# Two token tiles loaded by halves, one behind a weight tile, and work moved within and off VectorE's queue, in an attention and feed-forward kernel

## The chip, the cores and the metric

The kernel runs on one core of a Trainium2 chip. Its engines each have a queue of their own: TensorE (PE) multiplies and transposes, VectorE (DVE), ScalarE (ACT) and GpSimd (POOL) do elementwise work, and SyncE (SP) issues most of the transfers; ACT and POOL can issue transfers too. The metric is the device time of one execution in microseconds (us). A profiled execution also has a span, from its first instruction to its last.

## The reference, cut to what matters

```python
xn = layernorm(x)                                   # x: 1 x 2048 x 448
qkv = xn @ wqkv                                     # 448 x 1344; 16 heads of 28
# attention over 8 keys, 2 positions apart: idx = pos - (0, 2, ..., 14), masked where idx < 0
attn = softmax(where(mask, einsum("bhsd,bhswd->bhsw", q, kg) * 28 ** -0.5, -1e9))
s = einsum("bhsw,bhswd->bhsd", attn, vg).reshape(1, 2048, 448) @ wo
g = silu(gelu(xn @ w1 + b1) @ w2 + b2)              # 448 x 1792 and 1792 x 448
out = x + s * g
```

The kernel computes all of it in bfloat16 with float32 sums.

## The kernel before, in words

**Tiling.** The 2048 tokens, even positions first and odd ones behind, are 16 token tiles of 128 rows (in SBUF: `x_sb`). The 448 columns of the model are contracted in row tiles (`kt`) of 128, the last of 64. So `wqkv` comes in row tiles 0, 1 and 2 (`w_in[:, kt]`) and a last one of 64 rows (`w_in3`). The load of row tile 2 stands ahead of that of row tile 1.

**Stages.** For each token tile VectorE takes the statistics (`stats`: BN_STATS L354, BN_AGGR L358), gets the reciprocal deviation with ACT or POOL (`rstds`), and writes the normalized tile `xn` (L422) with a copy of its last 64 columns behind it (L427). It is turned into `xnT`: for tiles 0 to 3 by PE (L404, L437) with a copy out of PSUM by DVE or ACT (`copy`, L250 and L252), for the others by a transposing transfer that SP issues (`dma_T`, L301). From `xnT` PE makes rows of q and k (L513) and v (L536). They are cast out of PSUM by ACT (L250) or DVE (L252) into `qk_tok` or `qk_pair` and `v_tok`; the first two are turned into `qkT` by transfers, v is written to DRAM and read back as windows. The first products, for tiles 0 and 1, are ordered by row tile of the weights: 0, 2, 1, and the last (`first_batch`). The feed-forward is L589 (`ff1`) with a GELU on ACT (L593) and L615 or L641 (`ff2`), to which DVE adds the second bias (`y`, L657).

Attention works on blocks of queries. `keys` makes `kb`, the keys of a block masked by plane (L700 on DVE, L698 on ACT, two instructions each); `scores` multiplies them (L715), ACT takes the exp (`E`, L721), and DVE or POOL multiplies by the mask (L731); `values_sum` multiplies E with v (L746), and DVE divides (`rd` L757, `a` L762). `a` goes through DRAM into `oT`. `store` multiplies the output product (L780, L795) by the gate (`sg`, L803 or L805), adds x (`o`, L811) and sends it out (L815).

**What sets the order.** Every step is a task added to a plan with the engines it may run on. `ORDER` is the program: a list of task numbers, each with the letter of the engine that it goes to (P, V, A, G, S for PE, DVE, ACT, POOL, SP; D marks where a transfer may count as landed). `emit` writes the instructions in that order, so on each engine they run in it, one behind the other. Buffers (8 PSUM banks, 4 `xn`, 2 `y`, 2 `kb`, 2 `sg`, 3 `o`) are taken and given back at the places in the list. Products by pairs of 64 rows (`pair`) have a small signal between their halves, issued by POOL, SP or ACT.

At the start the list has eleven matmuls on constants (L265, ten of 512 columns and one of 128), which depend on no load. A transfer from SP or ACT uses one of eight semaphores in turn; the ninth waits until the first has landed.

Of the kernel before, what the change touches and what calls it, by code (L numbers as in the profile page):

```python
# [11 lines left out]
ACT = mybir.ActivationFunctionType  # L12
# [10 lines left out]
G140 D141 V152 P301 V153 G297 V91 S154 D155 P163 G302 V89 P298 V90 G164 V92 V87 G94 G264 G265 D266 P303 A300 V143 P165
V79 A305 S144 D145 P316 V194 A166 V198 A299 V195 G167 D168 P311 V199 S196 D197 V80 V88 V169 G317 G93 A304 P318 S200
D201 P306 A319 G312 V186 G170 D171 V187 V190 A320 G172 D173 P313 V191 S188 D189 G307 G174 D175 P156 V653 A314 G176
D177 V654 P308 A315 S192 D193 G157 G178 D179 P158 A310 P291 V159 A160 S256 D257 S258 D259 A309 P321 G292 S262 D263
G180 D181 S260 D261 P293 G322 G182 D183 P225 A294 P323 A295 G226 P227 A325 P267 P485 V229 A324 V273 S161 D162 P505
A228 G486 V275 V277 V279 P487 G506 V274 P495 A488 V276 V268 A489 P507 G496 V278 V280 P497 V282 A509 P475 V284 V286
A508 V283 V285 A498 P209 V288 G476 G210 V287 G281 A499 P477 V289 P216 V334 G217 G290 A478 V335 V338 S336 D337 P211
A479 V339 V330 P480 V213 S340 D341 V212 P218 V326 G481 P490 A219 V327 V331 S214 D215 A222 G220 D221 P482 G491 G223  # L30
D224 V683 P492 A484 S332 D333 V684 P500 A493 V412 A483 P202 V413 S328 D329 G501 A494 V400 P502 G203 V401 S402 D403
P204 A504 P655 V205 P580 A503 V206 S207 D208 S414 D415 A50 G248 D249 V408 G250 D251 V409 A656 V404 P239 A658 A581 V405
V657 V659 S410 D411 P582 G240 S230 D231 S406 D407 P660 V586 P685 A661 P241 V583 A663 P232 V245 V662 A686 P365 V713
V664 A688 G233 V714 A587 P234 A366 V687 V689 A242 P690 G923 V236 P367 A235 V588 P589 A691 S237 D238 G243 D244 A693
V692 V694 G246 D247 A584 S924 D925 A369 V585 S926 D927 A368 P715 S370 D371 G590 P695 P665 V696 A716 P591 V666 V697
A718 V667 V698 V668 V699 V669 G700 D701 P349 V592 G670 D671 S672 D673 P720 V595 A593 G350 P674 G702 D703 P351 V675
A721 G252 D253 V676 P416 A352 G254 D255 V353 A723 P342 G417 V677 S354 D355 V678 A596 P418 G343 V743 G679 D680 P704
V717 A420 P344 G681 D682 V705 A419 V706 P598 A346 S421 D422 V719 V707 A345 V708 V744 G709 D710 S347 D348 V597 G711
D712 P725 V722 G599 P745 V726 P750 V727 A746 P600 S928 D929 A748 V728 V729 A751 V724 G730 D731 S732 D733 A753 V594
V747 V749 P734 V604 P379 V735 A605 V736 P372 G380 V737 P381 V738 G373 P356 V601 G741 S739 D740 D742 A385 S930 D931  # L40
V773 A602 P755 G386 D387 P374 V756 G357 V382 P358 A375 V757 G383 D384 P430 A359 V774 A362 P446 G360 D361 V758 V759
G363 D364 P775 V376 S447 S760 D761 P448 G431 G762 D763 G388 D389 G392 D393 A776 V752 S377 D378 P780 A778 V449 P432
A781 V754 P423 S424 V803 A783 P764 V777 A450 P425 V765 A433 V766 P453 G390 D391 A436 V767 V768 P607 A427 V426 A454
S769 D770 G394 D395 V779 G396 D397 V804 G398 D399 V606 G434 D435 V603 G437 D438 P455 V782 G608 P439 V784 G771 D772
G271 D272 G269 D270 A459 V456 P805 G460 D461 V833 A440 P441 A806 G457 D458 V834 P785 A808 P609 V786 A443 V787 V788
V789 G463 D464 G465 D466 V442 S792 S428 D429 G790 D791 D793 V807 V809 S444 D445 G462 P810 V613 P540 A811 V610 A813
A541 P794 P815 V812 A51 G467 D468 P515 V795 V796 G469 D470 P542 V797 A516 V798 A611 P517 V816 G801 S799 D800 D802 V817
A544 P530 V818 A543 V819 P535 V814 A518 A531 G820 D821 V612 G822 D823 P824 A614 P532 A536 G471 D472 A519 V825 P537
V826 G473 D474 A534 P510 V827 V828 A539 V615 V863 P525 G829 D830 S831 D832 A533 A511 A538 P512 S526 A864 P520 P955
S521 S451 D452 A514 P527 G956 A513 P957 A528 P522 V958 V959 A529 P944 V962 A524 V963 P835 P840 A523 G945 S960 D961  # L50
P946 S964 D965 A52 P616 V947 V951 V952 A841 S953 D954 A843 V842 V948 A836 P865 V844 S949 D950 S934 D935 S932 D933 S936
D937 G617 P870 A838 V837 P618 A871 V839 A873 G872 A866 A868 V867 G874 A893 P845 V622 P625 G869 V846 V847 A623 V848
A894 V849 V619 G850 D851 V624 P854 G852 D853 A620 S626 P895 P627 V855 A896 V856 A898 V857 V858 V621 G859 D860 V897
G861 D862 V899 P550 V631 V628 P966 A632 G551 A629 V633 P900 G967 P977 A901 V630 A903 P968 V902 G978 A53 V904 P545 S938
D939 V973 P979 V974 G546 V969 S975 D976 P552 V980 G970 P905 A554 P547 V906 V907 S971 D972 A553 P555 V908 V981 A549
V909 S982 D983 P875 G556 P557 A548 V984 S910 D911 P884 S912 D913 V876 A559 P575 V877 A558 V885 P570 V886 S576 V887
V888 P577 S571 V878 G889 D890 P572 V879 A578 G891 D892 V985 P999 A579 G880 D881 S986 D987 P560 A574 G1000 G882 D883
# [66 lines left out]
def kernel(  # L124
# [13 lines left out]
    P = 128  # L138
# [17 lines left out]
    for v in range(9):  # L156
        n = NW - 1 if v == 4 else NW
# [23 lines left out]
    x_sb = sb("x_sb", [P, NT, D])  # L181
# [38 lines left out]
    p_st = ring("st", 4, [P, 6], F32)  # L220
# [38 lines left out]

    t_on = plan.add("DMA", lambda _: None, ())  # L260
    t_warm = t_on
    for n in (512,) * 10 + (P,):
        def idle(k, n=n):
            one = nc.const_aps
            nc.tensor.matmul(buf(p_b, k)[:, :n], one.tensor(1.0, [P, P], BF16), one.tensor(1.0, [P, n], BF16), start=True, stop=True)  # L265
        t_warm = plan.add("PE", idle, [t_warm], take=(p_b,))
        t_warm.give = ((p_b, t_warm, 0),)
# [18 lines left out]
    def dma(eng, dst, src, deps=()):  # L286
        def fn(_):
            {"SP": nc.sync, "ACT": nc.scalar, "POOL": nc.gpsimd}[eng].dma_start(dst, src)
        a = plan.add(eng, fn, [t_on] + list(deps))
        return plan.add("DMA", lambda _: None, [a])  # L290
# [61 lines left out]
    def stats(t):  # L352
        def f1(k):
            nc.vector.bn_stats(out=buf(p_st, k)[:], in_=x_sb[:, t, :])  # L354
# [578 lines left out]
    t = plan.add("POOL", None, [seen[b, 1][0] for b in range(2)])  # L933
# [43 lines left out]
```

## Time and profile before

| | |
|---|---|
| median of 3 runs | 149.83 us (149.45 to 150.26) |
| the profiled execution | 149.96 us |
| its span | 148.2 us |
| granted TensorE clock | 0.997 |
| instructions | 4658 |

A profile's row has the start in us, the length in us (merged rows: from the first start to the last end), engine and line, operation, output and inputs with their sizes, and the count; in brackets the idle time of the engine just before it and what ended it. A group's row has after the bar the busy us, the mean ns of one, and behind the second bar the idle time before them. A window's row has, for each engine, its busy us in that stretch, then PE's clock, the share of the DMA engines and GB/s. SPq is SP's queue: its transfers are listed by when they are issued and how long the issue takes. L12 is line 12 of the kernel.

### The profile page before, as it was taken

Reading aid. Unit: us, or ns where it says so; the run is one execution under the profiler, and the core shown is the slowest. Engines: PE = TensorE matmul, PEld = TensorE weight load, DVE = VectorE, ACT = ScalarE, POOL = GpSimd, SP = SyncE. Lnnn points to the kernel's source line nnn. Section 1 sums busy time; section 2 is a strip of 40 time slices with the busy share of each in tenths; the row PEclk is TensorE's granted clock in tenths of the full one; section 3 lists DMA queues with packets and bytes.
Section 4 is the critical chain, followed back from the end, with each engine's and each line's share of the span. In section 5 each row is a group of like instructions: output and inputs, shape, how many; then the busy total and the mean of one; then the engine's idle time right before and its main releaser. Section 6 shows DMA issues by size and latency. Waiting matters only on the chain.

```text
span 148.2 us, 4658 instructions
## 1 busy us (share of the span) xinstructions
PE 142.9 (96%) x1827; PEld 78.7 (53%) x1827; DVE 108.2 (73%) x302; ACT 89.2 (60%) x164; POOL 56.0 (38%) x112
## 2 busy tenths in 40 slices
PE   7899999999999899999999999999999999999991
PEld 2444555444455566666665554545665564545570
DVE  3789934198941997999999999627589997671642
ACT  4336676675782682645574539989874876571120
POOL 6753694007330021651389675600463024110200
PEclk9999999999999999999999999999999999999998
DMA  4999999999599899697489989952682332264112
GB/s 145 320 282 323 189 205 193 255 367 206 143 154 130 179 132 192 133 198 181 117 227 136 215 203 122 300 113 64 102 176 78 71 98 63 78 166 127 43 31 62
DMA packets 43966, 24.17 MB, mean 163 GB/s; under 512 B 33822, under 2 KB 42022, under 8 KB 43944
## 3 DMA queue, kind: packets, MB, share of 16 engines
q1 hardware_dynamic: 41080, 17.25, 59.4%
q0 software_dynamic: 2720, 6.51, 17.9%
q8 instruction: 14, 0.23, 0.7%
q10 hardware_dynamic: 144, 0.11, 0.2%
q14 instruction: 8, 0.07, 0.1%
HBM read 9.70 MB, written 6.29 MB: 108 GB/s over the span
## 4 chain that ended last, share of the span: by engine, by line
PE 64%; DMA 17%; DVE 12%; SPq 2%; issue 2%; POOL 1%; DVEq 0%
PE bank L615 18%; PE bank L589 14%; PE bank L513 10%; PE bank L641 7%; DMA xnT<-xn 6%; PE bank L780 5%; DMA w_in<-in_A_wqkv_dram 4%; DMA qkT<-qk_tok 4%; PE bank L536 4%; DVE st L354 3%; DMA x_sb<-in_A_x_dram 3%; PE bank L746 3%; PE bank L715 2%; DVE qk_tok L252 2%; PE bank L795 1%
## 5 line engine op out<-in xcount | busy, mean ns | idle before, releaser
L589 PE MATMUL bank<-xnT,w 64*128 64x512 bf16 x392 | 46.6, 376 | 0.0
L593 ACT ACTIVATE h<-bank,b 128x512 bf16<-128x512 f32 x56 | 35.2, 686 | 13.6 <-PE bank L589 13.2
L615 PE MATMUL bank<-w,h 64*128 64x448 bf16 x336 | 33.8, 349 | 0.0
L589 PEld LDWEIGHTS <-w 64*128 64x128 bf16 x392 | 19.7, 94 | 19.5 <-issue 0.6
L513 PE MATMUL bank<-w_in,xnT 64*128 64x448 bf16 (+1 forms) x212 | 26.3, 350 | 0.6 <-DVE y L657 0.4
L615 PEld LDWEIGHTS <-h 64*128 64x128 bf16 x336 | 17.1, 94 | 12.9
L721 ACT ACTIVATE E<-bank 128x456 bf16<-128x456 f32 (+1 forms) x36 | 17.4, 550 | 10.6 <-PE bank L715 9.5
L769 POOL DMA_DIRECT2D o_rows<-a x25 | 13.4, 538 | 26.4 <-DVE a L762 10.2
L762 DVE TENSOR_TENSOR a<-bank,rd 114x448 bf16<-114x448 f32 (+1 forms) x36 | 22.2, 622 | 1.1
L295 POOL DMA_DIRECT2D v<-v_rows x22 | 13.9, 637 | 7.0 <-PE bank L589 6.5
L513 PEld LDWEIGHTS <-xnT 64*128 64x128 bf16 (+1 forms) x212 | 10.9, 94 | 9.1 <-issue 1.2
L295 POOL DMA_DIRECT2D v_rows<-v_tok x16 | 9.1, 572 | 14.5 <-PE bank L715 9.4
L536 PE MATMUL bank<-w_in,xnT 64*128 64x448 bf16 (+1 forms) x106 | 13.8, 349 | 0.0
L657 DVE TENSOR_TENSOR y<-bank,b 128x448 f32<-128x448 f32 x15 | 9.0, 620 | 5.7 <-PE bank L641 4.8
L354 DVE BATCH_NORM_STATS2 st<-x_sb 128x6 f32<-128x448 bf16 x16 | 9.2, 610 | 3.9 <-DMA x_sb<-in_A_x_dram 3.9
L731 DVE TENSOR_TENSOR E<-E,m_gen 128x456 bf16<-128x456 bf16 (+1 forms) x29 | 10.8, 393 | 1.4 <-ACT E L721 1.4
L641 PE MATMUL bank<-w,h 128*128 128x448 bf16 (+2 forms) x70 | 11.4, 315 | 0.0
L669 ACT ACTIVATE t<-y 128x448 f32<-128x448 f32 x12 | 6.9, 579 | 7.3 <-DVE y L657 7.3
L700 DVE TENSOR_SCALAR kb<-qkT,plane 128x512 bf16<-128x512 bf16 x30 | 9.1, 352 | 2.8 <-DMA qkT<-qk_tok 1.9
L422 DVE TENSOR_SCALAR xn<-x_sb,mv,rstd 128x448 bf16<-128x448 bf16 x15 | 5.8, 393 | 6.2 <-DMA xnT<-xn 4.2
L250 ACT CAST v_tok<-bank 128x448 bf16<-128x448 f32 x12 | 6.2, 540 | 6.6 <-PE bank L536 4.2
L252 DVE CAST qk_tok<-bank 128x448 bf16<-128x448 f32 x11 | 6.5, 617 | 2.9 <-PE bank L513 2.9
(86 smaller groups left out, 170.7 us busy)
## 6 DMA issues: line engine op xcount, KB each, us to landing
v_rows<-v_tok POOLq DMA_DIRECT2D x16, 128.0 KB, 3.2
v<-v_rows POOLq DMA_DIRECT2D x14, 128.0 KB, 5.0
out_dram<-o SPq DMA_DIRECT2D x15, 112.0 KB, 1.7
w<-in_B_w_dram SPq DMA_DIRECT2D x2, 784.0 KB
o_rows<-a POOLq DMA_DIRECT2D x23, 64.1 KB, 3.2
w<-in_B_w_dram SPq DMA_DIRECT2D x2, 672.0 KB
x_sb<-in_A_x_dram SPq DMA_DIRECT2D x3, 448.0 KB, 7.2
w_in<-in_A_wqkv_dram SPq DMA_DIRECT2D x3, 336.0 KB, 4.9
```

The source lines that it names most:

```text
L295: nc.gpsimd.dma_start(dst(k), src())
L354: nc.vector.bn_stats(out=buf(p_st, k)[:], in_=x_sb[:, t, :])
L513: return nc.tensor.matmul(ps[:, :D], xnT[r, kt, cs], w, start=start, stop=stop)
L536: return nc.tensor.matmul(ps[:, :D], xnT[r, kt, k0:k0 + P], w, start=start, stop=stop)
L589: return nc.tensor.matmul(ps[:], w1[r, kt, ms], xnT[r, kt, cs], start=start, stop=stop)
L593: nc.scalar.activation(buf(p_h, own, i)[:], buf(p_b, own, i)[:], ACT.Gelu_apprx_tanh, bias=b1[:, mt:mt + 1])
L615: return nc.tensor.matmul(ps[:, :D], buf(*h_at[(c, mt)])[r, j * P:(j + 1) * P], w2[r, mt, :], start=start, stop=stop)
L641: nc.tensor.matmul(ps[:, :n], buf(*h_at[(c, mt)])[:, j * P:(j + 1) * P], w2[:, mt, cs], start=(mt == 0 and not biased), stop=(mt == NMT - 1))
L721: nc.scalar.activation(buf(p_E, k)[:, :n], buf(p_b, a, r)[:, :n], ACT.Exp, scale=SCALE)
L731: (nc.gpsimd if k.on == "POOL" else nc.vector).tensor_tensor(out=E, in0=E, in1=m, op=ALU.mult)
L762: nc.vector.tensor_tensor(out=o, in0=sums(k, e)[:, :, :, :DH], in1=buf(p_rd, rd)[rows].unsqueeze(2).unsqueeze(3).to_broadcast((2 * nq, 8, ...
L769: (nc.gpsimd if k.on == "POOL" else nc.sync).dma_start(o_rows[n + i * nq:n + i * nq + nq, :], buf(p_a, own)[i * nq:i * nq + nq, i, :])
```

## The change

It has two parts, in the loads at the start and in the list of tasks.

**Loads.** Token tiles 0 and 1 are each loaded by two transfers of 64 rows, the first half on SP and the second on ACT (before: tile 0 whole on SP, tile 1 whole on ACT). Tiles 2 and 3, one transfer before, are two, and that of tile 3 stands behind row tile 1 of the weights. The statistics of a tile wait for both of its halves. The matmuls on constants are ten instead of eleven.

SP's queue from the program's start, before the change (`w_in` 128x1344 is a row tile of `wqkv`, row tile 0 and then 2 in the second row and row tile 1 in the fourth; `w_in_65` the last row tile; `w_66` is `w1`):

```order
L288 DMA x_sb<-in_A_x_dram 128x448
L288 DMA w_in<-in_A_wqkv_dram 128x1344 x2
L288 DMA x_sb<-in_A_x_dram 128x2x448
L288 DMA w_in<-in_A_wqkv_dram 128x1344
L288 DMA w_in_65<-in_A_wqkv_dram 64x2x448
L288 DMA w_in_65<-in_A_wqkv_dram 64x896
L288 DMA w_66<-in_B_w_dram 128x3x896
```

And after it:

```order
L288 DMA x_sb<-in_A_x_dram 64x448 x2
L288 DMA w_in<-in_A_wqkv_dram 128x1344 x2
L288 DMA x_sb<-in_A_x_dram 128x448
L288 DMA w_in<-in_A_wqkv_dram 128x1344
L288 DMA x_sb<-in_A_x_dram 128x448
L288 DMA w_in_65<-in_A_wqkv_dram 64x2x448
L288 DMA w_in_65<-in_A_wqkv_dram 64x896
L288 DMA w_66<-in_B_w_dram 128x3x896
```

The load of two tiles has become one load before and one behind row tile 1, and two halves stand where one tile stood. ACT's queue begins with two halves instead of one tile.

**The list.** Two xn with their copies (V408 V409 and V404 V405 before) go behind the masks of the first exps, and the second of them behind the two y. Five casts (before V353, V382, V376, V426, V442) and three pairs of kb (V744, V804, V834) go from DVE to ACT, and one sum o (V959) from DVE to POOL. Since five more load tasks are made and one matmul task fewer, a task's number from the weights' later loads on is greater by 5.

DVE's queue at 45 to 51 us of the profile, before (`y_104` is the y that frees the bank of the next q product; `E<-E,m_first` are the first masks):

```order
L252 CAST qk_pair<-bank_159 128x16x28
L252 CAST qk_pair<-bank_161 128x16x28
L422 TENSOR_SCALAR xn<-x_sb,mv,rstd 128x448
L427 COPY xn<-xn 128x64
L422 TENSOR_SCALAR xn<-x_sb,mv,rstd 128x448
L427 COPY xn<-xn 128x64
L731 TENSOR_TENSOR E<-E,m_first 128x456 x2
L657 TENSOR_TENSOR y_104<-bank_156,b_72 128x448
L657 TENSOR_TENSOR y_105<-bank_155,b_72 128x448
L252 CAST v_tok_78<-bank_159 128x16x28
```

And after:

```order
L252 CAST qk_pair<-bank_158 128x16x28
L252 CAST qk_pair<-bank_160 128x16x28
L735 TENSOR_TENSOR E<-E,m_first 128x456 x2
L426 TENSOR_SCALAR xn<-x_sb,mv,rstd 128x448
L431 COPY xn<-xn 128x64
L661 TENSOR_TENSOR y_104<-bank_155,b_72 128x448
L661 TENSOR_TENSOR y_105<-bank_154,b_72 128x448
L426 TENSOR_SCALAR xn<-x_sb,mv,rstd 128x448
L431 COPY xn<-xn 128x64
L252 CAST v_tok_78<-bank_158 128x16x28
```

The masks stand first, and the y ahead of the second xn. The lines after the load helper are 4 greater; the bank numbers are shifted by one all through, since one matmul fewer takes a bank at the start.

ACT's queue at 61 to 69 us, before:

```order
L250 CAST qk_pair_150<-bank3_157 128x16x28
L721 ACTIVATE E_98<-bank7_161 128x456
L669 ACTIVATE t1_107<-y1_105 128x448
L250 CAST qk_tok1_152<-bank0_154 128x16x28
L250 CAST qk_tok1_152<-bank6_160 128x16x28
L250 CAST qk_pair_150<-bank4_158 128x16x28
L250 CAST qk_pair_150<-bank2_156 128x16x28
L721 ACTIVATE E_98<-bank3_157 128x456
```

And after:

```order
L250 CAST qk_pair_150<-bank2_156 128x16x28
L250 CAST qk_pair_150<-bank4_158 128x16x28
L725 ACTIVATE E_98<-bank6_160 128x456
L673 ACTIVATE t1_107<-y1_105 128x448
L250 CAST qk_tok1_152<-bank7_161 128x16x28
L250 CAST qk_tok1_152<-bank5_159 128x16x28
L250 CAST qk_pair_150<-bank3_157 128x16x28
L250 CAST qk_pair_150<-bank1_155 128x16x28
L702 ACTIVATE kb1_149<-qkT_74,plane_82 128x2x4x64 x2
L725 ACTIVATE E_98<-bank2_156 128x456
```

A second cast of `qk_pair` stands ahead of the first exp and a pair of kb ahead of the next four.

The diff, with a line of the list for the start:

```diff
 ORDER = """
-D0 A31 D32 G14 S29 D30 V12 P1 V13 V15 V19 V20 A48 V21 S33 D34 V22 V16 G45 V17 V18 P2 V23 G46 D47 S39 D40 P3 S35 D36
+D0 A30 D31 G13 S28 D29 S32 D33 A34 D35 V11 P1 V12 V14 V18 V19 A53 V20 S36 D37 V21 V15 G50 V16 V17 P2 V22 G51 D52 S44
...
     t_warm = t_on
-    for n in (512,) * 10 + (P,):
+    for n in (512,) * 9 + (P,):
...
+    def load_x_halves(t):
+        t_x[t] = [dma(eng, x_sb[r:r + 64, t, :], rows(x_half, t * P + r, 64), ()) for eng, r in (("SP", 0), ("ACT", 64))]
+
     def load_x(t0, n, eng="SP", deps=()):
         d = dma(eng, x_sb[:, t0:t0 + n, :], rows(x_half, t0 * P, n * P).rearrange("(t p) d -> p t d", p=P), deps)
         for t in range(t0, t0 + n):
-            t_x[t] = d
+            t_x[t] = [d]
...
-    load_x(0, 1, "SP")
-    load_x(1, 1, "ACT")
+    load_x_halves(0)
+    load_x_halves(1)
...
     load_w(0)
-    load_x(2, 2, "SP")
+    load_x(2, 1, "SP")
+    load_x(3, 1, "SP")
     load_w(1)
...
-        k = plan.add("DVE", f1, [t_x[t]], take=(p_st,))
+        k = plan.add("DVE", f1, t_x[t], take=(p_st,))
```

More of the change, by code (lines that the diff above doesn't have):

```diff
@@ L23 @@
[L23 to L57, printed above, removed]
@@ new lines @@
+V287 A514 P480 V289 V291 A513 V288 V290 A503 P214 V293 G481 G215 V292 G286 A504 P482 V294 P221 V339 G222 G295 A483
+V340 V343 S341 D342 P216 A484 V344 V335 P485 V218 S345 D346 V217 P223 V331 G486 P495 A224 V332 V336 S219 D220 A227
+G225 D226 P487 G496 G228 D229 V688 P497 A489 S337 D338 V689 P505 A498 V417 A488 P207 V418 S333 D334 G506 A499 V405
+P507 G208 V406 S407 D408 P209 A509 P660 V210 P585 A508 V211 S212 D213 S419 D420 A55 G253 D254 G255 D256 A661 P244 A663
+A586 V662 V664 V413 V414 S415 D416 P587 G245 S235 D236 P665 V591 P690 A666 P246 V588 V409 V410 S411 D412 A668 P237
@@ new lines @@
+V250 V667 A691 P370 V718 V669 A693 G238 V719 A592 P239 A371 V692 V694 A247 P695 G928 V241 P372 A240 V593 P594 A696
+S242 D243 G248 D249 A698 V697 V699 G251 D252 A589 S929 D930 A374 V590 S931 D932 A373 P720 S375 D376 G595 P700 P670
+V701 A721 P596 V671 V702 A723 V672 V703 V673 V704 V674 G705 D706 P354 V597 G675 D676 S677 D678 P725 V600 A598 G355
+P679 G707 D708 P356 V680 A726 G257 D258 V681 P421 A357 A358 G259 D260 A728 P347 G422 V682 S359 D360 V683 A601 P423
+G348 V748 G684 D685 P709 V722 A425 P349 G686 D687 V710 A424 V711 P603 A351 S426 D427 V724 V712 A350 A749 V713 G714
@@ new lines @@
+D715 S352 D353 V602 G716 D717 P730 V727 G604 P750 V731 P755 V732 A751 P605 S933 D934 A753 V733 V734 A756 V729 G735
+D736 S737 D738 A758 V599 V752 V754 P739 V609 P384 V740 A610 V741 P377 G385 V742 P386 V743 G378 P361 V606 G746 S744
+D745 D747 A390 S935 D936 V778 A607 P760 G391 D392 P379 V761 G362 P363 A387 A380 V762 G388 D389 P435 A364 V779 A367
+A381 P451 G365 D366 V763 V764 G368 D369 P780 S452 S765 D766 P453 G436 G767 D768 G393 D394 G397 D398 A781 V757 S382
+D383 P785 A783 V454 P437 A786 V759 P428 S429 V808 A788 P769 V782 A455 P430 V770 A438 V771 P458 G395 D396 A441 V772
@@ new lines @@
+V773 P612 A432 A431 A809 A459 S774 D775 G399 D400 V784 G401 D402 G403 D404 V611 G439 D440 V608 G442 D443 P460 V787
+G613 P444 V789 G776 D777 G276 D277 G274 D275 A464 V461 P810 G465 D466 V838 A445 P446 A811 G462 D463 P790 A813 P614
+V791 A448 A447 A839 V792 V793 V794 G468 D469 G470 D471 S797 S433 D434 G795 D796 D798 V812 V814 S449 D450 G467 P815
+V618 P545 A816 V615 A818 A546 P799 P820 V817 A56 G472 D473 P520 V800 V801 G474 D475 P547 V802 A521 V803 A616 P522 V821
+G806 S804 D805 D807 V822 A549 P535 V823 A548 V824 P540 V819 A523 A536 G825 D826 V617 G827 D828 P829 A619 P537 A541
@@ L63 @@
+V923 P572 S945 D946 V1011 G994 G926 P995 V1012 A573 P639 S1013 D1014 V1000 A574 S924 D925 D927 V996 A59 V1001 P640
+V997 S1002 D1003 S998 D999 P643 V641 A642 S947 D948 P1020 P644 P1015 V645 P647 A646 V1016 V1017 V1021 S1018 D1019 P648
+G1022 P651 S1023 D1024 V649 A650 P652 P1030 A653 P1025 V1031 V1032 P654 V1026 S1033 D1034 P655 P1035 V1027 A656 V1036
+S1028 D1029 V1037 S1038 D1039
 """
```

29 lines of the change are left out of this document (20 added, 9 removed).

## The prediction

> **What bounds the kernel now.** I read the page's totals first, then what TensorE (PE) waited for.
>
> ```profile
> PE 142.9 (96%) x1827; PEld 78.7 (53%) x1827; DVE 108.2 (73%) x302; ACT 89.2 (60%) x164; POOL 56.0 (38%) x112
> ...
> PE bank L513 <- DVE y L657: 0.4, 1, 0.4
> PE bank L404 <- DVE xn L391: 0.4, 1, 0.4
> PE bank L513 <- DMA w_in<-in_A_wqkv_dram: 0.2, 1, 0.2
> ```
>
> PE is busy for 142.9 of 148.2 us, and apart from its launch the second view has three waits, each met once. So an edit is worth what it takes from one of those, or from the start, or what it adds as a new wait. The listed waits are too short, because a matmul's row lasts about 0.35 us where the next follows after 0.19. I therefore measure a stall from start to start. The timeline of the first 11 us, with one row of the chain of waits (the transfer of 6.16) and the window of 5 to 10 us (its last figure is GB/s), gives the start:
>
> ```profile
> 0.84 3.98 PE L265 MATMUL bank<-const-bfloat16-1.0 128*128 128x512 bf16 x11 [0.84 <-PEq L961]
> 1.25 0.89 SPq L288 DMA_DIRECT2D w_in<-in_A_wqkv_dram  x2
> 2.66 6.16 DMA w_in<-in_A_wqkv_dram
> 3.32 0.63 DVE L354 BATCH_NORM_STATS2 st<-x_sb 128x6 f32<-128x448 bf16 x1 [1.41 <-DMA x_sb<-in_A_x_dram]
> 6.29 0.39 PE L437 MATMUL bank<-ident,xn 128*128 128x128 bf16 x4
> 6.65 0.39 SPq L288 DMA_DIRECT2D x_sb<-in_A_x_dram  x1
> 6.68 0.54 PE L513 MATMUL bank<-w_in,xnT 128*128 128x448 bf16 x2
> 7.92 0.63 DVE L354 BATCH_NORM_STATS2 st<-x_sb 128x6 f32<-128x448 bf16 x1 [1.02 <-DMA x_sb<-in_A_x_dram]
> 8.30 0.35 PE L536 MATMUL bank<-w_in,xnT 128*128 128x448 bf16 x1
> 8.68 0.60 DVE L354 BATCH_NORM_STATS2 st<-x_sb 128x6 f32<-128x448 bf16 x1
> 8.87 0.54 PE L513 MATMUL bank<-w_in,xnT 128*128 128x448 bf16 x2 [0.21 <-DMA w_in<-in_A_wqkv_dram]
> 9.38 0.40 DVE L422 TENSOR_SCALAR xn<-x_sb,mv,rstd 128x448 bf16<-128x448 bf16 x1
> 10.42 0.42 DVE L252 COPY xnT<-bank 128x512 bf16<-128x512 bf16 x1
> 10.90 0.93 PE L513 MATMUL bank<-w_in,xnT 64*128 64x448 bf16 x8
> 5.00:10.00 5.00, 4.51 (x28) 2.33 (x28) 3.57 (x16) 1.74 (x6) 3.84 (x16) 1.00 1.05 314
> ```
>
> At 6.68 PE starts the products with the weights' row tile 2. SP's issue at 6.65 waits for the same load, because it reuses that load's semaphore, so row tile 2 lands at about 6.64. At 8.87 PE starts row tile 1, which lands at 2.66 + 6.16 = 8.82; PE was free at 8.30 + 0.19 = 8.49, so this costs 0.38. Tiles 2 and 3 land together at about 7.9 and VectorE (DVE) takes their statistics one after the other, at 7.92 and 8.68. From there a chain without slack (xn at 9.38, copy of xnT at 10.42) releases PE at 10.90. After that PE runs gapless, but for some tenths, to 49.5.
>
> **The change, part by part: the loads.** The halves of tiles 0 and 1 put both queues on tile 0 first. The end that speaks for them is tile 0 landing up to 0.3 us before 3.3, since tile 1 no longer shares the engines with it; the other end is no gain. Either way PE then stands at 6.64 for row tile 2, so I price it at nothing on the path. The Trainium skill speaks against this edit: "DMA: Bandwidth & Descriptors", section Rules for kernel authors, says that two transfers to disjoint partition halves serialize on the same engines and that one 128-partition transfer should be used. By that rule tile 0 gains nothing and the extra issues are a pure loss: with 0.45 for them instead of the 0.1 below, the sum would be -0.21 instead of -0.56. No row of before shows one tile in two halves.
>
> SP issues one half more ahead of row tile 0, at 0.89 / 2 = 0.45 us each. The loads behind come between 0 later (the engines have a backlog: row tile 1 needs 6.16 us from issue to landing) and 0.45 later (none). I take 0.1, near the backlog's end. The ACT queue's second issue delays only its table load, and the square root for tile 0 comes long after.
>
> Row tile 1 now has one token tile less ahead of it: 128 x 448 x 2 bytes = 115 KB, at 314 GB/s 0.37 us. It lands at about 8.45, and PE's wait of 0.38 is gone. Tile 3, however, now stands behind it, with exactly the bytes ahead that row tile 1 has today, so it lands at about 8.82 instead of 7.9. Behind its statistics in DVE's queue stand the reciprocal, xn and copy of tile 2, and PE waits for these. The statistics move from 8.68 to 8.87, so the chain releases PE at 11.09 instead of 10.90: the 0.38 is eaten and 0.19 is lost. With the 0.1 of the issues: **+0.3**. The ends are -0.38 (tile 3 in time; the 0.38 is kept) and +0.64 (0.19 + 0.45).
>
> The missing warm-up matmul costs nothing: PE sits idle between the warm-up's end at 0.84 + 3.98 = 4.82 and the first transpose, waiting for xn (second row of the waits). Were that cover gone, it would save its 0.4.
>
> **DVE's order at 45 to 51 us.** The timeline:
>
> ```profile
> 44.58 0.97 ACT L721 ACTIVATE E<-bank 128x456 bf16<-128x456 f32 x2
> 45.62 0.40 DVE L422 TENSOR_SCALAR xn<-x_sb,mv,rstd 128x448 bf16<-128x448 bf16 x1 [1.92 <-DMA xnT<-xn]
> 45.89 2.81 PE L615 MATMUL bank<-w,h 64*128 64x448 bf16 x28
> 48.33 0.40 DVE L422 TENSOR_SCALAR xn<-x_sb,mv,rstd 128x448 bf16<-128x448 bf16 x1 [2.10 <-DMA xnT<-xn]
> 48.86 0.70 DVE L731 TENSOR_TENSOR E<-E,m_first 128x456 bf16<-128x456 bf16 x2
> 48.96 1.88 ACT L721 ACTIVATE E<-bank 128x456 bf16<-128x456 f32 x4 [3.40 <-PE bank L715]
> 48.98 0.73 PE L536 MATMUL bank<-w_in,xnT 64*128 64x448 bf16 x6
> 49.47 1.15 DVE L657 TENSOR_TENSOR y<-bank,b 128x448 f32<-128x448 f32 x2
> 50.14 2.07 PE L513 MATMUL bank<-w_in,xnT 64*128 64x448 bf16 x20 [0.43 <-DVE y L657]
> 50.75 1.25 SPq L301 DMA_TRANSPOSE xnT<-xn  x1
> ```
>
> The L513 row at 50.14 needs the bank that the first y empties. The y could read at 45.89 + 2.81 = 48.70, but xn at 48.33 and two masks at 48.86 stand ahead of it. PE's six products from 48.98 are three pairs at 0.19, so it was free at 49.55 and lost 0.59. After the change the masks (0.70, their exps done at 45.55) stand ahead of the xn at 45.62, which then ends its copy by 46.9, still within DVE's idle 2.10 before 48.33. So y starts at 48.75 and frees its bank at 49.37. The next bank comes from the first exp of the row at 48.96, at about 49.5. Gain 0.58; the ends are that and 0. The xn that goes behind the y's runs at 49.9 to 50.5 (0.40, then its 0.18 copy); SP takes its transpose at 50.75, so this is hidden. Less than 0.3 is left there: were it gone, later transposes would slip by the excess.
>
> **The sum o moved to POOL, at 100 us.**
>
> ```profile
> 100.23 0.39 DVE L811 TENSOR_TENSOR o<-x_sb,sg 128x448 bf16<-128x448 bf16 x1
> 100.54 0.62 DVE L805 SCALAR_TENSOR_TENSOR sg<-bank,g 128x448 bf16<-128x448 f32 x1
> 100.70 0.89 PE L715 MATMUL bank<-qkT,kb 64*128 64x57 bf16 x32
> 104.64 0.61 PE L715 MATMUL bank<-qkT,kb 64*128 64x57 bf16 x32
> L811 POOL TENSOR_TENSOR o<-x_sb,sg 128x448 bf16<-128x448 bf16 x2 | 2.1, 1030 | 13.4 <-DVE sg L803 8.7 <-DVE sg L805 4.7
> ```
>
> Two score groups take 0.61 us where nothing holds them and 0.89 at 100.70: the second waits 0.28 for the bank of the sg at 100.54. Without o ahead of it, sg starts 0.31 sooner. Gain 0.28, ends 0.28 and 0. POOL needs 1.03 instead of 0.39; it is idle there, and only a store waits for it.
>
> **Eight operations from DVE to ScalarE (ACT), 61 to 87 us:** five casts and three pairs of kb.
>
> ```profile
> L250 ACT CAST v_tok<-bank 128x448 bf16<-128x448 f32 x12 | 6.2, 540 | 6.6 <-PE bank L536 4.2
> L698 ACT ACTIVATE kb<-qkT,plane 128x512 bf16<-128x512 bf16 x6 | 4.0, 725 | 0.0
> 56.00:90.00 34.00, 34.00 (x609) 20.91 (x602) 32.46 (x88) 18.29 (x38) 18.65 (x32) 1.00 0.95 181
> 66.89 1.88 ACT L721 ACTIVATE E<-bank 128x456 bf16<-128x456 f32 x4 [2.04 <-PE bank L715]
> 75.89 1.85 ACT L721 ACTIVATE E<-bank 128x448 bf16<-128x448 f32 x4 [0.74 <-PE bank L715]
> 87.58 0.99 ACT L721 ACTIVATE E<-bank 128x456 bf16<-128x456 f32 x2 [2.30 <-PE bank L715]
> ```
>
> In this window PE is busy for all 34.00 us, so nothing is to be won directly. ACT gains at most 5 x 0.54 + 6 x 0.73 = 7.1 us beside 18.29 busy, and has 15.7 idle; before three of the exps that follow a moved operation it waits 2.04, 0.74 and 2.30 for PE. Price 0. What it buys is that DVE, 32.46 of 34 busy, can follow a PE that arrives earlier from 50 us on.
>
> **Sum:** +0.3 - 0.58 - 0.28 = -0.56. The profiled execution took 149.96 (span 148.2 and 1.76 around it), so 149.40 by it; it lies 0.13 above the median of 149.83, and against the median this is 149.27. I say 149.3.
>
> **Rivals.** *Tile 3 lands in time* (by 8.3): PE keeps the 0.38, total -1.24, 148.6. For it: 6.16 us for row tile 1 is slow against 314 GB/s (some engine lags, which may not come again). Against it: the same bytes in the same order. *PE finds another late release* at 50 and 101 us: the two gains vanish and 149.83 + 0.3 gives 150.1. Against it: both rows show PE free and only DVE late. *ACT's queue becomes the bound* (the other side): a moved cast (0.54) or kb pair (1.45) delays the exps behind it, at about 61, 66, 76 and 87 us. That is 3 x 0.54 + 1.45 = 3.1 at most; it decides from 0.9 us of delay reaching PE, and half of the most gives 149.3 + 1.5 = 150.8. Against it: the idle times above. *The clock stays low*: the eleven warm-up matmuls take 0.4 us each against 0.19 for the later ones, so PE starts slow, and a shorter warm-up may leave the first products slow. Doubling the 18 products of 0.19 between 5.7 and 10 us costs at most 3.4, less the waits there, 0.55: about +1.4 if half are hit, 150.7. The Trainium skill, "TensorE: Matmul & The Clock Gate", Part 1, says that the clock is released by a busy window of about 3.4 us which runs freely; by it ten matmuls (3.6 us) leave less margin than eleven, and no run here shows it yet.
>
> **How the numbers follow.** Forecast 43%, tile 3 in time 25%, another release 15%, ACT 12%, clock 5%. The forecast's own range is 148.9 to 149.7; with the rivals of either side, short of ACT and clock, the range is 148.5 to 150.3. This kernel's runs spread by half a per cent, so 0.5% (0.75 us) is what counts as a change. Faster: 25% and the lower quarter of the forecast, 35%. Slower: ACT and clock, 17%. Same: 48%.
>
> **What would show it.** Right: DVE's fourth statistics row starts at about 8.9 after a wait for x_sb; PE's wait for w_in is gone and one for xn or xnT stands at 10 to 11 us; no PE wait for y at 50; two L715 groups in 0.61 at 100. Wrong: the fourth statistics at 8.0 (first rival), or PE waits for E or kb between 60 and 90 (ACT).

## The result, and the profile after

The changed kernel takes 150.93 us (median of 5), the kernel before 149.75 beside it. The ratio of the means is 1.0114, 95% interval 1.0077 to 1.0151; the medians alone give 1.008, because one of the five runs took 152.70. So the changed kernel is slower by about 1%, outside the predicted range. In a later comparison, with twelve runs, the ratio was 1.0036 (1.0001 to 1.0071): slower both times, but the two intervals do not meet, so the size of the loss is not fixed by one comparison. A ratio leaves out runs that took over 1.5% more than the fastest of the same kernel. The profiled execution took 150.93 with a span of 149.2 at a granted clock of 1.0, against 149.96 and 148.2: a loss of 0.97.

First what was forecast to go away. The page's totals of the changed kernel, and what TensorE (PE) waited for:

```profile
PE 143.5 (96%) x1826; PEld 76.2 (51%) x1826; DVE 104.8 (70%) x290; ACT 95.3 (64%) x175; POOL 56.9 (38%) x113
...
PE bank L408 <- DVE xn L395: 0.5, 1, 0.5
PE bank L593 <- DMA xnT<-xn: 0.4, 1, 0.4
PE bank L441 <- DVE xn L426: 0.4, 1, 0.4
PE bank L517 <- DVE qk_pair L252: 0.3, 1, 0.3
```

The waits for y and for row tile 1 (`w_in`) are gone. Three new ones stand in their place: xn at L441, `xnT` of a transposing transfer at L593, and `qk_pair`.

To see what each stage cost I number PE's 1816 products behind the warm-up, which come in the same order in every kernel here but for a few that change places with a neighbour, and read from each trace when the k-th starts (us):

| product | before | after | after minus before |
|---|---|---|---|
| first | 5.16 | 5.24 | +0.08 |
| 61st | 13.20 | 13.83 | +0.63 |
| 121st | 19.49 | 20.37 | +0.88 |
| 181st | 25.73 | 27.19 | +1.46 |
| 201st | 28.15 | 30.08 | +1.93 |
| 401st | 47.03 | 48.96 | +1.93 |
| 501st | 53.20 | 54.55 | +1.35 |
| 1201st | 94.52 | 95.96 | +1.44 |
| 1301st | 102.18 | 103.34 | +1.16 |
| last | 144.70 | 145.87 | +1.17 |
| end of the span | 148.25 | 149.23 | +0.98 |

The loss is made by 30 us, 1.93 in all. Then 0.58 come back at 50 us and 0.28 at 101, just the two gains forecast. Between 54 and 95 us the moved casts and kb change it by 0.09.

**The start.** Queues of SP and ACT, first of the changed kernel, then of the kernel before (rows not shown yet):

```profile
0.79 1.19 ACTq L288 DMA_DIRECT2D x_sb<-in_A_x_dram  x2
0.80 1.46 SPq L288 DMA_DIRECT2D x_sb<-in_A_x_dram  x2
2.30 1.06 SPq L288 DMA_DIRECT2D w_in<-in_A_wqkv_dram  x2
6.18 1.78 SPq L288 DMA_DIRECT2D w<-in_B_w_dram  x3
8.00 0.59 SPq L288 DMA_DIRECT2D x_sb<-in_A_x_dram  x1
```

```profile
0.80 0.40 ACTq L288 DMA_DIRECT2D x_sb<-in_A_x_dram  x1
0.80 0.39 SPq L288 DMA_DIRECT2D x_sb<-in_A_x_dram  x1
2.66 1.90 SPq L288 DMA_DIRECT2D w_in<-in_A_wqkv_dram  x3
4.61 1.76 SPq L288 DMA_DIRECT2D w<-in_B_w_dram  x3
```

Two halves hold SP for 1.46 us (0.58 and 0.82, with a step between) where one whole tile held it for 0.39. Row tile 0 is issued at 2.30 instead of 1.25, 1.05 later and not 0 to 0.45. The first loads of w1 (`w`) are issued 1.57 later, tiles 4 to 7 1.35 later (6.65 before). By the trace's semaphore events the last of w1's six loads lands at 18.50 instead of 17.04. Tile 0 gains nothing: its halves land at 3.12 and 3.29, the whole tile landed at 3.30.

VectorE (DVE) and PE of the changed kernel, in the same stretch:

```profile
3.38 0.63 DVE L358 BATCH_NORM_STATS2 st<-x_sb 128x6 f32<-128x448 bf16 x1 [1.48 <-DMA x_sb<-in_A_x_dram]
7.00 0.63 DVE L358 BATCH_NORM_STATS2 st<-x_sb 128x6 f32<-128x448 bf16 x1
8.60 0.54 PE L517 MATMUL bank<-w_in,xnT 128*128 128x448 bf16 x2
9.08 0.63 DVE L358 BATCH_NORM_STATS2 st<-x_sb 128x6 f32<-128x448 bf16 x1 [1.23 <-DMA x_sb<-in_A_x_dram]
9.81 0.40 DVE L426 TENSOR_SCALAR xn<-x_sb,mv,rstd 128x448 bf16<-128x448 bf16 x1
10.26 0.45 PE L441 MATMUL bank<-ident,xn 128*128 128x128 bf16 x4 [0.37 <-DVE xn L426]
11.33 0.93 PE L517 MATMUL bank<-w_in,xnT 64*128 64x448 bf16 x8
```

Here the prediction's picture holds. PE starts row tile 1 at 8.60, just behind its landing at 8.56, and the waits above no longer list it. Tile 3's statistics wait for its load, at 9.08 (8.68 before), and tile 2's chain behind them releases PE at 11.33 instead of 10.90.

**From 12 to 30 us.** SP's transposing transfers, a DVE wait and PE, after, and then the rows of before that answer them:

```profile
12.60 8.77 SPq L301 DMA_TRANSPOSE qkT<-qk_tok  x3
21.46 5.28 SPq L301 DMA_TRANSPOSE xnT<-xn  x4
25.07 1.16 DVE L704 TENSOR_SCALAR kb<-qkT,plane 128x512 bf16<-128x512 bf16 x4 [3.07 <-DMA qkT<-qk_tok]
26.16 0.60 DVE L252 CAST qk_pair<-bank 128x448 bf16<-128x448 f32 x1
26.81 0.91 PE L517 MATMUL bank<-w_in,xnT 64*128 64x448 bf16 x7 [0.31 <-DVE qk_pair L252]
29.64 1.69 PE L593 MATMUL bank<-xnT,w 64*128 64x512 bf16 x14 [0.40 <-DMA xnT<-xn]
```

```profile
12.17 7.47 SPq L301 DMA_TRANSPOSE qkT<-qk_tok  x3
19.74 5.18 SPq L301 DMA_TRANSPOSE xnT<-xn  x4
23.09 1.15 DVE L700 TENSOR_SCALAR kb<-qkT,plane 128x512 bf16<-128x512 bf16 x4 [1.91 <-DMA qkT<-qk_tok]
27.71 1.47 PE L589 MATMUL bank<-xnT,w 64*128 64x512 bf16 x12
```

The first transposes start 0.43 later but the three hold SP for 8.77 instead of 7.47, so the four for xnT of tiles 4 to 7 begin 1.72 later. The last of these lands at 29.60, and PE starts at 29.64. In the profile of before it landed at 26.48 (25.88 to 27.58 in four profiles of that kernel). The third transpose also delays the kb, and behind them in DVE's queue the cast of `qk_pair` for which PE waits at 26.81. Both late waits have this one source.

**The two gains** (first y, then the score group behind sg):

```profile
50.67 1.16 DVE L661 TENSOR_TENSOR y<-bank,b 128x448 f32<-128x448 f32 x2 [2.22 <-PE bank L619]
51.48 1.86 PE L517 MATMUL bank<-w_in,xnT 64*128 64x448 bf16 x17
102.14 0.61 PE L719 MATMUL bank<-qkT,kb 64*128 64x57 bf16 x32
```

The y now waits for PE and not PE for the y, and the second score group takes 0.61 instead of 0.89.

### The profile page after: what moved, and what is told of

The parts are those of the page before. It is cut to its first block, busy times and chain, and to the rows that moved or that the text cites. A ratio compares the mean times of both kernels' runs of the same rounds, so it can differ in the third digit from the quotient of the medians.

```text
span 149.2 us, 4659 instructions
## 1 busy us (share of the span) xinstructions
PE 143.5 (96%) x1826; PEld 76.2 (51%) x1826; DVE 104.8 (70%) x290; ACT 95.3 (64%) x175; POOL 56.9 (38%) x113
## 4 chain that ended last, share of the span: by engine, by line
PE 77%; DMA 12%; SPq 4%; DVE 3%; POOL 1%; issue 1%; DVEq 0%
PE bank L593 21%; PE bank L619 21%; PE bank L517 10%; PE bank L645 7%; PE bank L540 5%; PE bank L784 5%; DMA x_sb<-in_A_x_dram 5%; DMA qkT<-qk_tok 5%; SPq L288 4%; DMA xnT<-xn 3%; PE bank L750 3%; PE bank L719 3%; PE bank L799 1%; DVE sg L807 1%; DVE st L358 1%
## 5 line engine op out<-in xcount | busy, mean ns | idle before, releaser
L593 PE MATMUL bank<-xnT,w 64*128 64x512 bf16 x392 | 47.6, 376 | 0.5 <-DMA xnT<-xn 0.4
L593 PEld LDWEIGHTS <-w 64*128 64x128 bf16 x392 | 19.8, 94 | 20.8 <-DMA w<-in_B_w_dram 1.2
L517 PE MATMUL bank<-w_in,xnT 64*128 64x448 bf16 (+1 forms) x212 | 26.9, 350 | 0.3 <-DVE qk_pair L252 0.3
L619 PEld LDWEIGHTS <-h 64*128 64x128 bf16 x336 | 16.0, 94 | 14.0
L540 PE MATMUL bank<-w_in,xnT 64*128 64x448 bf16 (+1 forms) x106 | 14.1, 349 | 0.0
L704 DVE TENSOR_SCALAR kb<-qkT,plane 128x512 bf16<-128x512 bf16 x24 | 7.5, 358 | 4.4 <-DMA qkT<-qk_tok 3.1
L815 POOL TENSOR_TENSOR o<-x_sb,sg 128x448 bf16<-128x448 bf16 x3 | 3.1, 1031 | 17.1 <-DVE sg L807 8.7
L761 DVE RECIPROCAL rd<-bank 114x8 f32<-114x8 f32 (+1 forms) x36 | 7.1, 200 | 2.6 <-PE bank L750 2.4
```

What stands on the lines that cost most here:

```text
L517: return nc.tensor.matmul(ps[:, :D], xnT[r, kt, cs], w, start=start, stop=stop)
L540: return nc.tensor.matmul(ps[:, :D], xnT[r, kt, k0:k0 + P], w, start=start, stop=stop)
L593: return nc.tensor.matmul(ps[:], w1[r, kt, ms], xnT[r, kt, cs], start=start, stop=stop)
L619: return nc.tensor.matmul(ps[:, :D], buf(*h_at[(c, mt)])[r, j * P:(j + 1) * P], w2[r, mt, :], start=start, stop=stop)
```

## The experiments

**Which part loses.** Four kernels divide the change into its list and its two edits of the loads, always with ten warm-up matmuls.

The list alone, with the loads of before:

```diff
-    load_x_halves(0)
-    load_x_halves(1)
+    load_x(0, 1, "SP")
+    load_x(1, 1, "ACT")
...
-    load_x(2, 1, "SP")
-    load_x(3, 1, "SP")
+    load_x(2, 2, "SP")
```

> The changed kernel with the loads of before (tiles 0 and 1 whole, tiles 2 and 3 in one transfer ahead of row tile 1), but its list of VectorE, ScalarE and POOL work, and ten warm-up matmuls. Theory (all of the loss is in the loads, the list gains its 0.59 at 50 us and its 0.28 at 101 us): 149.75 - 0.87 = 148.9. Rival (the list gives its gains back, by casts and kb on ScalarE that delay exps): 149.5 to 150.5.

Ratio to before 0.9987 (0.9954 to 1.0019); the profiled execution 149.02. By the interval the list loses at most 0.2% and gains at most half of a per cent. The theory's 0.87 us would be a ratio of 0.994, which lies outside it.

The loads alone: the lines of the changed kernel with the order of the list before.

```diff
 ORDER = """
-(the list after)
+(the list before, with the loads at the start in the order of after)
```

> The changed kernel's loads and ten warm-up matmuls, with the list of before. Theory: 150.93 + 0.87 = 151.8, with the waits at 50 and 101 us back. Rival (the list gives its gains back elsewhere): 150.9, as the changed kernel.

Ratio 1.012 (1.0074 to 1.0167): all of the loss, and as much as list and loads together (1.0114). The reason stands in PE's rows at 50 and 101 us of this kernel:

```profile
50.77 2.25 PE L517 MATMUL bank<-w_in,xnT 64*128 64x448 bf16 x22
101.32 0.89 PE L719 MATMUL bank<-qkT,kb 64*128 64x57 bf16 x32
```

At 50 us there is no wait, though the y still stand behind the xn as in the list before: PE comes 1.2 us later, and the y is done by then. The 0.28 at 101 us is still there. So the 0.58 is not a gain that adds to any loss at the start.

The two edits of the loads, each without the other: the halves with tiles 2 and 3 together again (`load_x(2, 2, "SP")` in place of the two loads), and tile 3 behind row tile 1 with tiles 0 and 1 whole again (`load_x(0, 1, "SP")`, `load_x(1, 1, "ACT")`).

> The changed kernel with tiles 2 and 3 in one transfer ahead of row tile 1 again; the halves stay. Theory (the longer and more numerous issues delay every load behind them, and this is most of the loss): the delay of about 1 us in the loads of w1 and of tiles 4 to 7 stays, 150.1 to 150.6. Rival (tile 3 behind row tile 1 is most of it): 149.2.

> The changed kernel with tiles 0 and 1 whole again; tile 3 stays alone behind row tile 1. Theory (the halves' issues are most of the loss): 148.9 plus the 0.2 to 0.4 of tile 2's chain waiting for tile 3's statistics = 149.1 to 149.3, and SP's issues behind the first at most 0.45 later than before. Rival (tile 3's place is most of it): 150.4 or more.

The halves: 1.0075 (1.0047 to 1.0103). Tile 3 alone: 0.9981 (0.9955 to 1.0006), no different from the list alone. So the loss hangs on the halves. The first theory expected 0.2 to 0.4 us for tile 3, which also was wrong: with tiles 0 and 1 whole, row tile 1 landed at 7.61 and tile 3 at 8.18, its statistics started at 8.20, and PE passed its 61st product at 12.80 (13.14 with the list alone). SP's queue and PE's late wait in the kernel with the halves:

```profile
0.80 1.45 SPq L288 DMA_DIRECT2D x_sb<-in_A_x_dram  x2
2.30 1.06 SPq L288 DMA_DIRECT2D w_in<-in_A_wqkv_dram  x2
20.81 5.20 SPq L301 DMA_TRANSPOSE xnT<-xn  x4
28.81 2.98 PE L592 MATMUL bank<-xnT,w 64*128 64x512 bf16 x26 [0.39 <-ACT h L596]
```

The last row names an h, but by the trace the last xnT landed at 28.67 and PE's queue passed its wait for it at 28.70. The h that ended last (at 28.69) is not what PE needed: with halves of columns, further down, PE starts the same product 0.30 before that h ends.

**Why SP is late: two queues at once, one transfer more, or the 64 rows.** Two kernels on the list after, with tiles 2 and 3 together. In the first, SP issues just what it did before, and ACT brings tile 1 by two halves of 64 rows:

```diff
-        t_x[t] = [dma(eng, x_sb[r:r + 64, t, :], rows(x_half, t * P + r, 64), ()) for eng, r in (("SP", 0), ("ACT", 64))]
+        t_x[t] = [dma(eng, x_sb[r:r + 64, t, :], rows(x_half, t * P + r, 64), ()) for eng, r in (("ACT", 0), ("ACT", 64))]
...
-    load_x_halves(0)
+    load_x(0, 1, "SP")
     load_x_halves(1)
```

> The changed list with ten warm-up matmuls and the loads of before, but tile 1 comes by two transfers of 64 rows, both issued by ACT; SP issues what it issued before. Theory (the loss is SP's later issues): SP issues row tile 0 by 1.3 and the time is that of the changed list with the loads of before, within 0.3 of it, so about 149.0. Rival (two queues that issue at once lengthen each other's issues, or 64-row transfers move more slowly): SP's issues of 0.40 and 0.43 go to 0.55 or more, row tile 0 is issued at 1.6 or later, and the time is 149.5 or more.

SP's queue in it, ACT's, and the wait at the start:

```profile
0.80 0.40 SPq L288 DMA_DIRECT2D x_sb<-in_A_x_dram  x1
1.25 0.89 SPq L288 DMA_DIRECT2D w_in<-in_A_wqkv_dram  x2
0.79 1.18 ACTq L288 DMA_DIRECT2D x_sb<-in_A_x_dram  x2
5.12 0.63 DVE L357 BATCH_NORM_STATS2 st<-x_sb 128x6 f32<-128x448 bf16 x1 [1.37 <-DMA x_sb<-in_A_x_dram]
6.22 0.62 PE L407 MATMUL bank<-ident,xn 128*128 128x128 bf16 x3 [1.28 <-DVE xn L394]
```

SP is not slowed by ACT's two issues beside it: 0.40, and row tile 0 at 1.25. ACT's own take 0.54 and 0.61. So the rival that two issuing queues lengthen each other falls for this case. The time (1.0042, 0.9993 to 1.009, with runs spread from 149.56 to 153.82) decides nothing, because the kernel has a fault of its own: tile 1's second half, issued at 1.36 behind row tile 0, lands at 5.02, and its statistics stand in DVE's queue ahead of tile 0's xn, so PE starts at 6.22.

In the second, SP brings tile 1 whole behind tile 0, and ACT brings none:

```diff
-    load_x_halves(0)
-    load_x_halves(1)
+    load_x(0, 1, "SP")
+    load_x(1, 1, "SP")
```

> The changed list with ten warm-up matmuls and the loads of before, but tile 1 whole is issued by SP, behind tile 0; ACT issues no load at the start. So SP has one more issue of 128 rows ahead of row tile 0, none of 64 rows. Theory (the number of SP's issues ahead of the weights and their length count): an issue of 0.43 more, row tile 0 issued at 1.7 instead of 1.25 (the halves made it 2.30), so somewhat under half of the halves' loss of 1.4: 149.4 to 149.6. Rival (only the halves' own form costs): 149.0.

0.9976 (0.9937 to 1.0016): the delay of 0.46 (row tile 0 at 1.71) costs nothing that shows. The theory's 149.4 to 149.6 would have been 1.001 to 1.003 of the 149.22 it was reckoned on, at the interval's end; the loss is not in proportion to the delay. Part of the reason is that tile 0, alone on its way, lands at 2.88 instead of 3.3, and PE starts at 4.75.

The same halving with another form tells the rest. Each tile comes by two halves of columns, 128 rows each, on the same queues and in the same number:

```diff
-        t_x[t] = [dma(eng, x_sb[r:r + 64, t, :], rows(x_half, t * P + r, 64), ()) for eng, r in (("SP", 0), ("ACT", 64))]
+        t_x[t] = [dma(eng, x_sb[:, t, c:c + 224], rows(x_half, t * P, P)[:, c:c + 224], ()) for eng, c in (("SP", 0), ("ACT", 224))]
```

> The changed list, ten warm-up matmuls, tiles 2 and 3 together; tiles 0 and 1 by halves on both queues, but halves of columns: 128 rows of 448 bytes instead of 64 rows of 896. Theory (a 64-row transfer takes longer to issue): issues of 0.40 to 0.45, row tile 0 issued at 1.7 instead of 2.30, landings and time as with tile 1 whole on SP, 0.998 of before. Rival (two transfers per tile cost as such, whatever their form): row tile 0 at 2.1 or later, 1.005 of before or more.

0.9961 (0.9931 to 0.9991), a little faster than before. Its queue and the wait at 28 us:

```profile
0.80 0.90 SPq L288 DMA_DIRECT2D x_sb<-in_A_x_dram  x2
1.74 0.91 SPq L288 DMA_DIRECT2D w_in<-in_A_wqkv_dram  x2
19.44 5.20 SPq L301 DMA_TRANSPOSE xnT<-xn  x4
27.31 4.49 PE L592 MATMUL bank<-xnT,w 64*128 64x512 bf16 x40
```

Two halves hold SP for 0.90 (0.40 and 0.44) instead of 1.45, the transposes for xnT start 1.37 sooner, and PE loses 0.1 us at this place instead of 0.5. Tile 0 lands at 3.00, sooner than whole beside tile 1 (3.30), and PE starts at 4.94. So the form of 64 rows is the cause of the loss, not the halving. Against whole tiles with the same list (0.9987, 0.9954 to 1.0019) the intervals overlap, so a gain by halves of columns is not shown.

**Is SP's lateness all of it?** Tiles whole, but two loads more on SP ahead of row tile 0, of 64 bytes a row, which nothing reads:

```diff
+    spare = sb("spare", [P, 2, 32])
+    for j in range(2):
+        dma("SP", spare[:, j, :], rows(x_half, 0, P)[:, 32 * j:32 * j + 32])
```

> The changed list with ten warm-up matmuls and the loads of before (tiles 0 and 1 whole), but two loads more on SP between tile 0 and row tile 0, each 128 rows of 64 bytes into a tile that nothing reads: 0.9 us of SP's queue and almost no bytes. Theory (the halves cost by making SP late): row tile 0 is issued at 2.15 (halves: 2.30), the last part of w1's weights lands at 17.5 or later (16.4 without), the last xnT of tiles 4 to 7 at 28.5 or later (26.5 without), PE passes 28 us 0.9 to 1.2 late, and the time is 0.5 to 0.8% over the kernel before, as with the halves. Rival (the halves' own 64-row transfers cost, not SP's lateness): landings within 0.4 of those without, time 0.998 of before.

The profile agrees with the theory, the time only in part. Row tile 0 is issued at 2.18 and w1 lands at 18.01; the transposes and PE:

```profile
2.18 0.91 SPq L288 DMA_DIRECT2D w_in<-in_A_wqkv_dram  x2
21.20 5.28 SPq L301 DMA_TRANSPOSE xnT<-xn  x4
29.91 1.90 PE L595 MATMUL bank<-xnT,w 64*128 64x512 bf16 x16 [0.81 <-ACT qk_tok L250]
```

Each step of the chain is late as with the halves (the last xnT lands at 29.77, and PE starts at 29.91, though the row names a cast), with whole tiles. But the ratio is 1.0013 (0.9978 to 1.0049), and the profiled execution, with 151.18, is long for this kernel, whose median is 150.06. So the delay and the halves were run again on one chip, beside two more kernels. In one only tile 0 is halved by rows and tile 1 is whole on ACT:

```diff
-    load_x_halves(1)
+    load_x(1, 1, "ACT")
```

The other is the changed kernel with only the form of the four halves changed to columns.

> The kernel with two loads of 64 bytes a row more on SP again, beside the halves on one chip. Theory (SP's lateness is the loss): its ratio to before and that of the halves agree within 0.3%. Rival (the 64-row form costs as well): the halves 0.4% or more above it.

> The changed kernel with tiles 2 and 3 together ahead of row tile 1 and the halves of 64 rows, again, beside the delay on one chip. Theory (SP's lateness is the loss): within 0.3% of the kernel with the two extra loads. Rival (the 64-row form costs as well): 0.4% or more above it.

> The changed list, ten warm-up matmuls, tiles 2 and 3 together; tile 0 by two halves of 64 rows, one on SP and one on ACT, tile 1 whole on ACT behind its half. SP has no issue more than before, only one of 0.57 instead of 0.40. Theory (SP's lateness is the loss): row tile 0 issued at 1.45, the last xnT of tiles 4 to 7 at 27.3 or before, the time 0.998 of before. Rival (the 64-row form costs in itself): 1.003 or more.

> The changed kernel with nothing altered but the form of the four halves: 128 rows of 224 columns instead of 64 rows of 448. Theory (the length of SP's issues decides): row tile 0 issued at 1.74 instead of 2.30, and the time 0.996 to 0.999 of before instead of 1.004 to 1.011, less than 0.4% from the version with tiles 2 and 3 together (0.9961). Rival (tile 3 behind row tile 1 adds its 0.3 us): 0.998 to 1.000.

The delay 1.0036 (0.9998 to 1.0074), the halves 1.0065 (1.0024 to 1.0107): 0.3% apart, with intervals that overlap over most of their width. The list alone had 0.9987, so SP's lateness alone comes to 0.3 to 0.5% and the halves to 0.8 to 0.9%. Both intervals of the delay overlap that of the list alone (0.9954 to 1.0019), so its loss is shown by the landings and not by the times alone. Whether the 64-row form costs something beyond the lateness stays open. Tile 0 alone by halves: 0.9991 (0.9949 to 1.0033), too wide to tell the two apart, though it does not reach the halves' 1.0065. Its queue is the surprise:

```profile
0.80 0.58 SPq L288 DMA_DIRECT2D x_sb<-in_A_x_dram  x1
1.43 1.28 SPq L288 DMA_DIRECT2D w_in<-in_A_wqkv_dram  x2
```

Here row tile 0, a transfer of 128 rows, took 0.81 to issue behind a 64-row one on both queues. So the second issue's 0.82 in the changed kernel is not explained by its own 64 rows; what lengthens it stays open. (This execution took 153.35, far above the kernel's median of 150.10, but its first issue of 0.58 is that of the other kernels with 64-row halves.)

The changed kernel with column halves issues row tile 0 at 1.71 and takes 0.9963 (0.9924 to 1.0002): with the same number of transfers on the same queues and tile 3 in its new place, the loss of 0.4 to 1.1% is gone. This and the version with tiles 2 and 3 together (0.9961) are the best found: 0.4% ahead of before (the interval of the first just reaches 1), and 0.7 to 1.5% ahead of the changed kernel by its two ratios.

**The two kernels beside each other again**, for the size of the gains at 50 and 101 us:

> The kernel before, for its trace on this chip. Theory: its stall for y at 50 us is there where PE comes to it at 49.5, and that of 0.28 at 101 us always.

> The changed kernel again, beside the others: 1.1% over the kernel before, so 150.9 for 149.2, and 0.3 to 0.6 over the version with tiles 2 and 3 together that was tried before (150.4).

> The kernel before, a third profile. Theory: its stall for y at 50 us depends on when the transposing transfers free xn; where the run is at 149.0, the stall is shorter than 0.58 or the start is earlier; the rows from 52 to 100 us take the same time.

> The kernel before, a fourth profile, with the same expectation as the third: the stall at 50 us shorter where the run is fast.

The changed kernel had 1.0036 here, less than forecast. Over the 401st to 501st product four profiles of before took 6.17, 6.15, 5.59 and 5.58 us, those of the changed kernel and of all kernels with its list 5.58 or 5.59. So the stall for y was there in two of four executions. Where it is missing, the rows show why (fourth profile; DVE and PE):

```profile
46.96 0.40 DVE L422 TENSOR_SCALAR xn<-x_sb,mv,rstd 128x448 bf16<-128x448 bf16 x1 [1.06 <-DMA xnT<-xn]
48.40 1.16 DVE L657 TENSOR_TENSOR y<-bank,b 128x448 f32<-128x448 f32 x2 [0.22 <-PE bank L615]
49.21 2.25 PE L513 MATMUL bank<-w_in,xnT 64*128 64x448 bf16 x22
```

The second xn waited only 1.06 us for a transposing transfer to free its buffer, where it waited 2.10 in the profile that the prediction read; then the masks and the y follow in time. That the run without the stall would be the fast one was wrong: this execution took 150.12, because it lost 1.0 us more at 99 us (the 1201st to 1301st product took 8.65, and 7.66 in the first profile). One profile does not show a run's usual losses.

PE's passing times in the kernels on which the verdict rests (us):

| product | list alone | loads alone | halves | delay | column halves |
|---|---|---|---|---|---|
| first | 5.24 | 5.24 | 5.24 | 5.17 | 4.94 |
| 61st | 13.14 | 13.78 | 13.35 | 13.11 | 12.60 |
| 201st | 28.09 | 29.37 | 29.24 | 30.34 | 27.74 |
| 501st | 52.55 | 53.83 | 53.70 | 54.80 | 52.20 |
| 1301st | 101.24 | 102.80 | 102.40 | 103.50 | 100.90 |
| end of the span | 147.30 | 148.69 | 148.34 | 149.46 | 146.85 |

What separates them is there by the 201st product, at 28 to 30 us. Only loads alone loses more behind it, the 0.28 at 101 us. Each column is one execution. The second profiles of the halves and of the delay passed the 201st product at 28.67 and 29.22, the changed kernel's at 30.43, and the four of before at 27.81 to 28.44, so the size of the loss varies. Its first step does not: in each of the eighteen profiles the last load of w1 lands at 17.24 or later where row tile 0 is issued at 2.18 or later, and by 17.04 where it is issued at 1.74 or earlier.

## Why the prediction was wrong

- **The issues: this step failed.** "SP issues one half more ahead of row tile 0, at 0.89 / 2 = 0.45 us each", between 0 and 0.45 later, taken as 0.1. Row tile 0 came 1.05 later. The 0.45 is the price of a 128-row issue, and the change adds 64-row ones. Their price stood in the profile of before: the row at 2.66 has three issues in 1.90, and the two with 64 rows took 0.74 and 0.59. Two issues of about 0.6 against one of 0.39 would have given an upper end of 0.8 instead of 0.45.
- **The backlog that was to hide the issues.** It was taken from row tile 1's 6.16 us to landing, and so far it held: row tiles 2 and 1 landed at 6.67 and 8.56, against 6.64 and 8.82 before. It does not reach to w1 and tiles 4 to 7, whose loads are issued 1.35 to 1.57 later and land 1.3 to 1.5 later, and after them SP's transposes. The prediction followed the loads to 11 us, where PE was 0.43 late; by 30 us it was 1.93. The term of +0.3, whose upper end was +0.64, measured +1.93 between the two first profiles, and +1.22 in loads alone (29.37 against 28.15): this is the mis-sized term. The prediction said "ACT queue's second issue delays only its table load", which held (the table load at 2.02 for 1.23). It took for granted that PE would run gapless "but for some tenths" behind 11 us as in the profile of before, which did not hold.
- **Tile 3 behind row tile 1.** The rows came as forecast (statistics at 9.08 for 8.87, PE released at 11.33 for 11.09, no listed wait for row tile 1). But alone, without the halves, its place cost nothing (0.9981), so the first rival, tile 3 in time, was nearer for this edit.
- **The halves on tile 0.** No gain, as priced. The Trainium skill, "DMA: Bandwidth & Descriptors", Rules for kernel authors, advises against such halves, and the trace agrees: tile 0 lands at 3.29 for 3.30. The sum worked out by it, -0.21, still took the wrong issue price. The skill adds, in Issuing engines are not separate DMA queues of that page, that the time to initiate a transfer "is usually small relative to the DMA itself". Here the first half's issue takes 0.58 of the 2.49 us from its start to its landing, and two hold SP for 1.46.
- **The order at 45 to 51 us, -0.58:** measured -0.58 between the 401st and 501st product of the two first profiles. But it is not a fixed term: the stall is missing in two of four profiles of before, and also in loads alone, where PE comes 1.2 later. That it came out to the hundredth is in part luck, since a profile without the stall would have given nothing, and adding it to a term for the loads was not right.
- **o on POOL, -0.28,** and **eight operations to ACT, 0:** measured -0.28, and +0.09 from 53 to 96 us. The first is there in every profile of before (7.66 us or more over the 1201st to 1301st product, 7.38 in the changed kernel). The rivals of a late release and of ACT's queue did not come.
- **The warm-up and the clock:** the granted clock is 1.0 and the products at 8.60 take what they took before; that rival did not come.

## What to carry to other kernels

Price an added transfer by the issue time of a row of the same form (here 64 rows 0.5 to 0.8 us, 128 rows 0.4, and 0.6 for the load of four tiles), and follow the issuing queue to all that it issues later, here the transposing transfers 20 us on, not only to the loads next in line. To split a tile's load over two queues, split its columns and keep 128 rows. A stall of an in-order engine that waits for transfers is worth its length only in executions that have it and only if nothing ahead of it makes the other engine late; take it from more than one profile.

## What was not expected of the hardware

- A transfer to 64 partitions takes longer to issue than one to 128 with twice the bytes: 0.54 to 0.61 on ACT against 0.40, 0.58 on SP against 0.39. By columns, with half the bytes and 128 rows, it takes 0.39 to 0.46, and 0.42 to 0.44 with 64 bytes a row: here the rows and not the bytes make the difference.
- When both queues begin with such a transfer, the issue after it takes 0.59 to 0.61 on ACT and 0.81 to 0.82 on SP, also where it has 128 rows. Beside a 128-row one on SP, ACT's 64-row ones did not lengthen SP's (0.40).
- Three transposing transfers hold SP for 6.4 to 9.2 us. In all eighteen profiles but one (3.8) the third one's issue ends 2.3 to 3.2 us behind the landing of w1's last load (17.04 and 19.65 before, 18.50 and 21.37 after, 18.01 and 21.11 with the delay). That the loads' bytes hold the transposes up is read from this agreement; it was not tried by taking the loads away.
